# Beacon attention and soft MoE on one core: slot inputs always with x stationary, a later right half, wider zero fill, 0.72 weights a pair

## The chip, the cores and the metric

The kernel runs on one core of a Trainium2 chip. Its time is device microseconds of one execution. The engines are TensorE (PE, with its weight loads as PEld), VectorE (DVE), ScalarE (ACT), GpSimd (POOL) and SyncE (SP); sixteen DMA engines move data between HBM and the core's memory. SP and POOL issue transfers here: SP's go into the profile's queue q1 (hardware), POOL's into q0 (software).

## What is computed

Attention over 8 batches and 8 heads, 576 tokens of 64 columns, with 16 beacon keys and values that every token sees and a causal mask over the rest. Its output, with the heads side by side, is x: 4608 rows of 512. A soft mixture of 8 experts follows:

```python
x = np.ascontiguousarray(attn_out.transpose(0, 2, 1, 3)).reshape(B * S, H * D)
logits = x @ phi                                    # 4608 x 32 slots
d = np.exp(logits - logits.max(0)); d /= d.sum(0)   # over the tokens
slot_input = (d.T @ x).reshape(E, 4, 512)
for e in range(E):                                  # w1 512x1024, w2 1024x512
    slot_out[e] = np.maximum(slot_input[e] @ w1[e], 0.0) @ w2[e]
c = np.exp(logits - logits.max(1)); c /= c.sum(1)   # over the slots
return c @ slot_out                                 # 4608 x 512
```

## The kernel before, in words

**Pairs.** Attention goes over 32 pairs of heads (NP), four pairs to a batch. The order of the work is written out by hand: `lists[n]` (L583 to L598) names the pieces of pair n, `do` (L609) runs them, and each engine takes its instructions in that order. Q and K of a pair are transposed on PE and copied by DVE (`transp4`: Qa, Qb, Ka, Kb; `transp`: Ta, Tb). S0 to S3 (`score`) are the four steps of scores: products into one of two PSUM tiles sc, an exponential on ACT (L403) into ex, and masks on POOL (L387). M is a mask on DVE (L413). A0 and A1 (`attend`) multiply the pair before with V into av, of which there is one; after A1 DVE takes reciprocals (L434) and writes the normalized rows into xb (L435), two buffers of one batch each.

**Slots.** When a batch of x is done, X0, X12 and X34 transpose it (L471, L476), L0 and L1 form its logits and their exponentials (L486, L490), and D turns those into dT, tokens on the partitions (L540 to L544). SI adds d.T @ x of a batch, two batches behind the pair that runs it. In it batches 0 to 5 go through `si_moving` (L560): the 128x32 block of dT is stationary, 512 columns of x move, four row blocks go to four groups of 32 columns of PE, and one DVE instruction adds the 128x512 sum to siq (L568). In pair 30, SX (`si_turn`, L571) folds the four groups and transposes with eight fp32 products against the selector slc, and DVE writes siacc (L576). Batches 6 and 7 go through `si_piece` (L546): blocks of 128 columns of x are stationary, 32 columns of dT move, 20 products, and one DVE instruction adds the 128x128 sum to siacc, already transposed (L556); the last one writes siT, which the first expert layer takes.

**Loads.** SP loads q, k (`load_pair`, six pairs ahead, five buffers each) and v (`load_r`, `load_vl`). The weights are 32 blocks of 1 MB, cast from 32 to 16 bits on the way by transfers that POOL issues (`load_w`, L190): 27 whole tiles w, then ten pieces wx into the buffers that q and k have left, of which the last six hold the left halves and then the right halves of the last three blocks (L209). How many are issued by which pair is `want(n)` (L667), looked at before S0 of each pair (L698), and at D in the last. Before D of the last pair POOL clears hTz (L696), a view of one of the V buffers in which the transposed hidden rows are put later.

**End.** After the pairs: logits and slot inputs of the last batch, `layer1` with ReLU on ACT and DVE, `turn` (hidden rows transposed into hTz, L784), `layer2` for experts 0 to 5. `slot_out(hf)` (L797) does experts 6 and 7 for one half of the columns and writes soh (L800). `group(cg, o, w)` (L831) makes 512 output rows: per row block a product (L838), an eviction by ACT (L840) or DVE (L843), and a transfer of two row blocks at a time by SP (L847, L850). There are nine groups: the left halves of the first three, with slot_out(1) ahead of the third, then their right halves, then six groups of full width.

**Start.** `late_constants` (L317) clears siq (DVE, L318), builds slc (POOL, L319, L321) and ssel (POOL).

Of the kernel before, what the change touches and what calls it, by code (L numbers as in the profile page):

```python
# [8 lines left out]
FP = mybir.dt.float32  # L9
F16 = mybir.dt.float16  # L10
BF = mybir.dt.bfloat16
AL = mybir.AluOpType
# [5 lines left out]
def kernel(  # L18
# [12 lines left out]
    nc = tc.nc  # L31
    P = 128
    B, H, S, D = q.shape
    Nb = beacon_k.shape[2]
    E, Dm, F = moe_w1.shape
    NSL = moe_phi.shape[1]
# [3 lines left out]
    NCH = 5  # L40
    UL = U - 4 * P
    UE = (UL + Nb) // 2
    J = S // 64
    NP = B * H // 2
    NDC = Dm // P
# [31 lines left out]
    POS = [0, 2, 1, 3, 4]  # L77
# [9 lines left out]
    const = ctx.enter_context(tc.tile_pool(name="const", bufs=1))  # L87
# [87 lines left out]
    NV = NW + 3  # L175
    wv = {}
    homes = ["qf", "kf"] * 5
    NH = len(homes)
# [50 lines left out]
    def dcols(x, c):  # L229
        o = 2 * P * (c // 2) + c % 2  # L230
        return x[:, o:o + 2 * P - 1:2]
# [70 lines left out]
    siT = const.tile([P, NDC, NSL], F16, name="siT")  # L302


    siq = const.tile([P, Dm], FP, name="siq")
    slc = const.tile([P, NSL], FP, name="slc")


    ssel = const.tile([P, E // EG, EG * SPE], F16, name="ssel")
    phih = const.tile([P, NDC, 4, NSL], F16, name="phih")  # L310
    bkT = const.tile([P, NP, Nb], BF, name="bkT")
# [3 lines left out]
    scs = [ps_sc.tile([P, 2, 512], FP, name=f"sc{i}") for i in range(2)]  # L315

    def late_constants():  # L317
        nc.vector.memset(siq[:, :], 0.0)  # L318
        nc.gpsimd.memset(slc[:, :], 0.0)  # L319
        for c in range(P // NSL):  # L320
            nc.gpsimd.affine_select(out=slc[:, :], in_=slc[:, :], compare_op=AL.not_equal, fill=1.0,  # L321
                                    base=-NSL * c, pattern=[[-1, NSL]], channel_multiplier=1)
        nc.gpsimd.memset(ssel[:, :, :], 0.0)
        for gr in range(E // EG):
            for i in range(EG):
                nc.gpsimd.affine_select(
                    out=ssel[:, gr, i * SPE:(i + 1) * SPE], in_=ssel[:, gr, i * SPE:(i + 1) * SPE],
                    compare_op=AL.not_equal, fill=1.0,
                    base=-(NSL * i + (gr * EG + i) * SPE), pattern=[[-1, SPE]], channel_multiplier=1)
# [216 lines left out]
    def si_piece(b):  # L546
        sp = ps_tr.tile([P, NDC, NSL], FP, name="tr", tag="tr")
        for t in range(NDC):
            for i in (1, 2, 3, 4, 0):
                m = P if i < 4 else UL  # L550
                nc.tensor.matmul(
                    sp[:, t, :],
                    dcols(xb[b % 2][0:m, POS[i], :, :].rearrange("p h d -> p (h d)"), t),
                    dT[b][0:m, i, :], start=(i == 1), stop=(i == 0))

        nc.vector.scalar_tensor_tensor(  # L556
            out=siT[:, :, :] if b == B - 1 else siacc[:, :, :], in0=sp[:, :, :],
            scalar=2.0 ** -8, in1=siacc[:, :, :], op0=AL.mult, op1=AL.add)

    def si_moving(b):  # L560
        sp = ps_tr.tile([P, Dm], FP, name="tr", tag="tr")
        for i in range(NCH):
            m, c = P if i < 4 else UL, i % 4
            nc.tensor.matmul(  # L564
                sp[NSL * c:NSL * c + NSL, :], dT[b][0:m, i, :],
                xb[b % 2][0:m, POS[i], :, :].rearrange("p h d -> p (h d)"),
                start=i < 4, stop=i in (1, 2, 3, 4))
        nc.vector.scalar_tensor_tensor(out=siq[:, :], in0=sp[:, :], scalar=2.0 ** -8,  # L568
                                       in1=siq[:, :], op0=AL.mult, op1=AL.add)

    def si_turn():  # L571
        sp = ps_tr.tile([P, NDC, NSL], FP, name="tr", tag="tr")
        for t in range(NDC):
            nc.tensor.matmul(sp[:, t, :], dcols(siq, t), slc[:, :],
                             start=True, stop=True)
        nc.vector.tensor_copy(out=siacc[:, :, :], in_=sp[:, :, :])  # L576

# [13 lines left out]
    lists[NP - 5] = "S1 A0 L0 M S2 Ka Kb S3 A1 X34 e0 S0".split()  # L594
    lists[NP - 4] = "S1 A0 L1 M S2 Ta Tb S3 e1 A1 d1 S0".split()
    lists[NP - 3] = "S1 D A0 SI M S2 Ta Tb S3 A1 X0 S0".split()
    lists[NP - 2] = "S1 A0 X12 M S2 X34 A1 L0 S3 SX S0".split()
    lists[NP - 1] = "S1 A0 P0 M S2 P1 A1 L1 S3 D".split()  # L598
    routing = {"X0": lambda b: xt_piece(b, (0,)), "X12": lambda b: xt_piece(b, (1, 2)),
               "X34": lambda b: xt_piece(b, (3, 4)), "L0": lambda b: logit_piece(b, 0),  # L600
               "L1": lambda b: logit_piece(b, 1), "D": lambda b: dt_piece(b),
               "SI": lambda b: (si_moving if b < B - 2 else si_piece)(b)}


    def idle_work(t, m):
# [3 lines left out]
    def do(n, w):  # L609
        b, g = divmod(n, H // 2)  # L610
        if w in routing:
            rb = b - 1
            if w == "SI" or n < NP - 1 and w in ("L1", "D"):
                rb = b - 2
            if rb >= 0:
                routing[w](rb)
        elif w in ("Qa", "Qb", "Ka", "Kb"):
            transp4(n // 2 + 1, "QK".index(w[0]), "ab".index(w[1]))
        elif w[0] == "T":
            m, ws = (n + 2, ("ab".index(w[1]),)) if w[1] in "ab" else (int(w[1]), (0, 1))  # L620
            for x in ws:
                transp(m, x)
        elif w == "BC":
            beacon_cast(1, B)
        elif w == "BT":
            beacon_t(1, B)
        elif w == "M":
            mask_f(n)
        elif w == "SX":
            si_turn()  # L630
        elif w[0] == "P":
            xt_pair(int(w[1]))
        elif w[0] == "A":
            if n >= 1:
                attend(n - 1, int(w[1]))
        elif w == "S0":
            if n + 1 < NP:
                score(n + 1, 0)
        elif w[0] == "S":
            score(n, int(w[1]))  # L640
        elif w == "bv":
            cast_bv0()
        elif w[0] in "cde":

            vb = 0 if n < 2 else b if g == 0 else b + 1
            if vb >= B:
                pass
            elif w[0] == "e":
                cast_vl(vb, int(w[1]))
            elif w[0] == "c":  # L650
                cast_r(vb, int(w[1]), nc.vector if vb == 0 else nc.gpsimd)
            else:
                dup(vb, int(w[1]))
# [12 lines left out]

    def want(n):  # L667
        if n < 24:
            return max(0, int(0.75 * n - 0.8))
        return {24: 18, 25: 20, 26: 21, 27: 23, 28: 25, 29: NV, 30: NV + 3}.get(n, NV + NH)  # L670

    transp(0, 0, nc.scalar.copy)
    beacon_cast(0, 1)
# [10 lines left out]
    for n in range(NP):  # L684
        b, g = divmod(n, H // 2)
        if n + 2 < NP and n not in (2, 3):
            beacon_k_in(n + 2, nc.gpsimd)
        for w in lists[n]:
            if n == 3 and w == "M":
                beacon_k_in(n + 1, nc.gpsimd)  # L690
                beacon_k_in(n + 2, nc.gpsimd)
            if n == 6 and w == "M":
                for r in range(4):
                    nc.vector.tensor_copy(out=phih[:, :, r, :], in_=phif[:, :, :])
            if n == NP - 1 and w == "D":
                nc.gpsimd.memset(hTz, 0.0)  # L696
            if w == ("e0" if n == 3 else "D" if n == NP - 1 else "S0"):
                while wl < want(n):  # L698
                    load_w(wl)
                    wl += 1  # L700
            do(n, w)
        for what, vb in asks.get((n, 0), []):
            what(vb)
        for m in (5, 6) if n == 0 else (n + 6,):
            if m < NP:
                load_pair(m)
        for what, vb in asks.get((n, 1), []):
            what(vb)
# [119 lines left out]
    sc_scope.close()  # L828
    ps_f = ctx.enter_context(tc.tile_pool(name="ps_f", bufs=4, space=PSUM, side="right"))

    def group(cg, o, w):  # L831
        dst = out[cg * P * G:(cg + 1) * P * G, :].rearrange("(p j) d -> p j d", j=G)
        for j0 in range(0, G, 2):
            osb = wh.tile([P, 2, Dm], FP, name="osb", tag="w")
            for j in range(j0, j0 + 2):
                i = cg * G + j
                fp_ = ps_f.tile([P, Dm], FP, name="fp", tag="fp")
                nc.tensor.matmul(fp_[:, 0:w], etok(cg, j), soh[:, o:o + w], start=True, stop=True)  # L838
                if j % 2 == 0:
                    nc.scalar.activation(osb[:, j - j0, o:o + w], fp_[:, 0:w], AF.Copy,  # L840
                                         scale=rc[:, i:i + 1])
                else:
                    nc.vector.tensor_scalar(out=osb[:, j - j0, o:o + w], in0=fp_[:, 0:w],  # L843
                                            scalar1=rc[:, i:i + 1], scalar2=None, op0=AL.mult)

                if cg == 0 and o == 0 and j0 == 0:
                    nc.sync.dma_start(out=dst[:, j:j + 1, o:o + w],  # L847
                                      in_=osb[:, j - j0:j - j0 + 1, o:o + w])
            if cg > 0 or o > 0 or j0 > 0:
                nc.sync.dma_start(out=dst[:, j0:j0 + 2, o:o + w], in_=osb[:, :, o:o + w])  # L850


    NL = 3
    for cg in range(NL):
        if cg == NL - 1:
            slot_out(1)
        group(cg, 0, HD)
    for cg in range(NL):
        group(cg, HD, HD)
    for cg in range(NL, NG):  # L860
# [31 lines left out]
```

## Time and profile before

| | |
|---|---|
| runs, us | 194.15, 195.35, 202.19; median 195.35 |
| profiled execution, us | 195.3 |
| its span, us | 193.6 |
| granted TensorE clock | 0.972 |
| PE, DVE, ACT, POOL busy, us | 156.8, 146.6, 129.5, 119.1 |
| DMA | 56.11 MB as landed, mean 290 GB/s |

The span runs from the first to the last instruction of the profiled execution; times in the text without another name count from its start. In the groups a line is: line, engine, operation, out<-in with shapes and count, then for a source or tile view least, median and longest duration in ns. The busy share of the DMA engines is shown in tenths for 40 slices of the span, as a sum over transfers that may overlap on an engine, so that it can be above 1.

### The profile page before, as it was taken

Reading aid. Unit: us, or ns where it says so; the run is one execution under the profiler, and the core shown is the slowest. Engines: PE = TensorE matmul, PEld = TensorE weight load, DVE = VectorE, ACT = ScalarE, POOL = GpSimd, SP = SyncE. Lnnn points to the kernel's source line nnn. Section 1 sums busy time; section 2 is a strip of 40 time slices with the busy share of each in tenths; the row PEclk is TensorE's granted clock in tenths of the full one; section 3 lists DMA queues with packets and bytes.
Section 4 is the critical chain, followed back from the end, with each engine's and each line's share of the span. In section 5 each row is a group of like instructions: output and inputs, shape, how many; then the busy total and the mean of one; then the engine's idle time right before and its main releaser. Section 6 shows DMA issues by size and latency. Waiting matters only on the chain.

```text
span 193.6 us, 7169 instructions
## 1 busy us (share of the span) xinstructions
PE 156.8 (81%) x2985; PEld 110.3 (57%) x2985; DVE 146.6 (76%) x306; ACT 129.5 (67%) x190; POOL 119.1 (62%) x278
## 2 busy tenths in 40 slices
PE   2569996989998989999998999999889999688300
PEld 1327674666676756767665766677567867343000
DVE  3595999989898988889898987997776524599500
ACT  3474876878788878879877877888668131399400
POOL 7996597678478858856875888697756860000000
PEclk9999999999999999999999999999999999999855
DMA  5999999999999999999999999999999999999995
GB/s 182 324 334 367 374 349 294 290 325 242 282 275 346 285 260 314 312 305 263 370 287 271 299 295 311 259 261 225 215 216 212 210 203 197 198 362 407 419 420 232
DMA packets 45048, 56.11 MB, mean 290 GB/s; under 512 B 4191, under 2 KB 30295, under 8 KB 45015
## 3 DMA queue, kind: packets, MB, share of 16 engines
q1 hardware_dynamic: 36359, 38.87, 58.7%
q0 software_dynamic: 8656, 16.78, 46.5%
q8 instruction: 23, 0.38, 0.7%
q14 instruction: 10, 0.08, 0.1%
HBM read 62.98 MB, written 9.44 MB: 374 GB/s over the span
## 4 chain that ended last, share of the span: by engine, by line
DVE 48%; PE 26%; issue 6%; DMA 5%; POOL 4%; ACT 3%; DVEq 0%; POOLq 0%; ACTq 0%
DVE xb L435 12%; PE av L426 9%; DVE qT L377 9%; DVE kT L377 8%; DMA wx<-in_moe_w_dram 5%; PE sc L396 4%; PE tr L375 4%; PE tr L486 4%; DVE ex L413 3%; DVE osb L843 3%; DVE kT L362 2%; DVE siq L568 2%; DVE qT L362 2%; ACT ex L403 2%; PE tr L564 2%
## 5 line engine op out<-in xcount | busy, mean ns | idle before, releaser
L403 ACT ACTIVATE ex<-sc 128x928 f16<-128x928 f32 (+2 forms) x128 | 106.4, 868 | 28.0 <-PE sc L396 20.6
L387 POOL TENSOR_SCALAR_AFFINE_SELECT ex<-ex 128x256 f16<-128x256 f16 x128 | 51.3, 414 | 35.4 <-ACT ex L403 32.8
L426 PEld LDWEIGHTS <-ex 128*128 128x128 f16 (+1 forms) x960 | 42.2, 106 | 18.2 <-issue 17.5
L396 PE MATMUL sc<-qT,kT 64*64 64x128 bf16 (+3 forms) x640 | 46.1, 264 | 4.8 <-DVE kT L382 2.2
L426 PE MATMUL av<-vh,ex 128*128 128x65 f16 x819 | 42.1, 199 | 0.1
L396 PEld LDWEIGHTS <-kT 64*64 64x64 bf16 (+1 forms) x640 | 17.6, 104 | 20.9 <-issue 7.9
L426 PE MATMUL av<-vd,ex 128*128 128x130 f16 x126 | 21.9, 225 | 8.7 <-DVE xb L435 6.6
L435 DVE TENSOR_TENSOR xb<-av,r 128x640 f16<-128x640 f32 (+1 forms) x32 | 26.0, 814 | 1.1
L377 DVE COPY kT<-tr 128x640 bf16<-128x640 bf16 (+1 forms) x24 | 18.0, 772 | 4.0 <-PE tr L375 4.0
L377 DVE COPY qT<-tr 128x640 bf16<-128x640 bf16 (+1 forms) x24 | 17.5, 769 | 3.2 <-PE tr L375 3.2
L413 DVE TENSOR_TENSOR ex<-ex,fmask 128x672 f16<-128x672 f16 x32 | 19.1, 595 | 0.4 <-ACT ex L403 0.2
L840 ACT ACTIVATE osb<-fp,rc 128x256 f32<-128x256 f32 (+1 forms) x24 | 12.9, 579 | 7.3 <-PE fp L838 6.7
L441 POOL CAST vh<-vr 128x1024 f16<-128x1024 f32 x15 | 16.0, 1066 | 0.1
L843 DVE TENSOR_SCALAR osb<-fp,rc 128x256 f32<-128x256 f32 (+1 forms) x24 | 13.7, 614 | 0.7 <-PE fp L838 0.6
L457 POOL CAST vh<-vl 48x256 f16<-48x256 f32 x32 | 13.2, 413 | 1.3
L838 PE MATMUL fp<-soh,eLh 128*128 128x256 f16 (+1 forms) x48 | 11.4, 325 | 2.6 <-ACT osb L840 1.5
L476 DVE COPY xT<-tr 128x512 f16<-128x512 f16 (+1 forms) x21 | 10.6, 504 | 0.9 <-PE tr L471 0.9
L471 PE MATMUL tr<-idh,xb 128*128 128x128 f16 (+1 forms) x140 | 10.8, 215 | 0.4 <-DVE qT L377 0.4
L375 PE MATMUL tr<-idb,kf 128*64 128x128 bf16 x216 | 9.9, 224 | 0.8 <-DVE qT L377 0.8
L838 PEld LDWEIGHTS <-eLh 128*128 128x128 f16 x48 | 5.3, 114 | 8.3 <-issue 6.5
L486 PE MATMUL tr<-xT,phih 128*128 128x288 f16 x56 | 9.2, 286 | 0.0
L375 PEld LDWEIGHTS <-kf 128*64 128x64 bf16 x216 | 7.1, 109 | 3.5 <-issue 3.3
(122 smaller groups left out, 199.3 us busy)
## 6 DMA issues: line engine op xcount, KB each, us to landing
w<-in_moe_w_dram POOLq DMA_DIRECT2D x27, 512.0 KB, 8.8
qf<-in_q_dram SPq DMA_DIRECT2D x32, 288.0 KB, 7.4
kf<-in_k_dram SPq DMA_DIRECT2D x32, 288.0 KB, 6.2
vr<-in_v_dram SPq DMA_DIRECT2D x15, 512.0 KB, 6.6
out_dram<-osb SPq DMA_DIRECT2D x12, 512.0 KB, 5.7
out_dram<-osb SPq DMA_DIRECT2D x11, 256.0 KB, 3.0
wx<-in_moe_w_dram POOLq DMA_DIRECT2D x10, 256.0 KB, 9.8
vl<-in_v_dram SPq DMA_DIRECT2D x16, 96.0 KB, 10.2
```

The source lines that it names most:

```text
L375: nc.tensor.transpose(tp[64 * r:64 * r + 64, j - j0, :], ts[r][:, j, :].bitcast(BF)[:, 1::2], idb[:, :])
L377: nc.vector.tensor_copy(out=dst[:, :, Nb:Nb + S].rearrange("p a (s j) -> p a s j", j=J)[:, :, :, j0:j1], in_=tp[:, :, :].rearrange("p j (a ...
L387: nc.gpsimd.affine_select(out=x, in_=x, compare_op=AL.is_ge, fill=0.0, base=base, pattern=pattern, channel_multiplier=cm)
L396: nc.tensor.matmul(sc[p0:p0 + kn, a, col:col + un], kT[n // 2 % 2][64 * a:64 * a + 64, n % 2, k0:k0 + ks * (kn - 1) + 1:ks], qT[n // 2 % 2 ...
L403: nc.scalar.activation(x[:, :, o:o + w], sc[:, :, 0:w], AF.Exp, scale=scale)
L413: nc.vector.tensor_tensor(out=x, in0=x, in1=fmask[:, :].unsqueeze(1).broadcast_to([P, 2, XT + UL]), op=AL.min)
L426: nc.tensor.matmul(dst, ex[n][0:kn, a, o:o + m], rhs, start=j in first, stop=j in final)
L435: nc.vector.tensor_tensor(out=xb[b % 2][:, :, h0:h0 + dh * (na - 1) + 1:dh, :].rearrange("p i a d -> p a i d"), in0=avv[:, :, :, 0:D], in1 ...
L441: eng.tensor_copy(out=vh[b % 2][:, 2 * r:2 * r + 2, :, 0:D].rearrange("p s h d -> p h s d"), in_=vr.pop((b, r))[:, :, :].rearrange("p h (s ...
L486: nc.tensor.matmul(lp[:, 0:w], phih[:, t, :, :].rearrange("p r e -> p (r e)"), xT[b][:, t, Nb + hf * w:Nb + (hf + 1) * w], start=(t == 0), ...
L838: nc.tensor.matmul(fp_[:, 0:w], etok(cg, j), soh[:, o:o + w], start=True, stop=True)
L843: nc.vector.tensor_scalar(out=osb[:, j - j0, o:o + w], in0=fp_[:, 0:w], scalar1=rc[:, i:i + 1], scalar2=None, op0=AL.mult)
```

## The change

All batches take `si_piece`, so `si_moving`, `si_turn`, the piece SX and the constants siq and slc go, and POOL clears siacc at the start. hTz is cleared through a view of 32-bit words. `want` asks for 0.72 weights a pair where it asked for 0.75, and for one less at pairs 24 and 25. `group` takes the row blocks as an argument, and in the third left group slot_out(1) stands between its two halves.

```diff
-    siq = const.tile([P, Dm], FP, name="siq")
-    slc = const.tile([P, NSL], FP, name="slc")
     def late_constants():
-        nc.vector.memset(siq[:, :], 0.0)
-        nc.gpsimd.memset(slc[:, :], 0.0)
-        for c in range(P // NSL):
-            nc.gpsimd.affine_select(out=slc[:, :], in_=slc[:, :], compare_op=AL.not_equal, fill=1.0,
-                                    base=-NSL * c, pattern=[[-1, NSL]], channel_multiplier=1)
+        nc.gpsimd.memset(siacc[:, :, :], 0.0)
...
-    def si_moving(b):
...
-    def si_turn():
...
-    lists[NP - 2] = "S1 A0 X12 M S2 X34 A1 L0 S3 SX S0".split()
+    lists[NP - 2] = "S1 A0 X12 M S2 X34 A1 L0 S3 S0".split()
...
-               "SI": lambda b: (si_moving if b < B - 2 else si_piece)(b)}
+               "SI": lambda b: si_piece(b)}
...
     def want(n):
         if n < 24:
-            return max(0, int(0.75 * n - 0.8))
-        return {24: 18, 25: 20, 26: 21, 27: 23, 28: 25, 29: NV, 30: NV + 3}.get(n, NV + NH)
+            return max(0, int(0.72 * n - 0.8))
+        return {24: 17, 25: 19, 26: 21, 27: 23, 28: 25, 29: NV, 30: NV + 3}.get(n, NV + NH)
...
-                nc.gpsimd.memset(hTz, 0.0)
+                nc.gpsimd.memset(hTz.bitcast(FP), 0.0)
...
-    def group(cg, o, w):
+    def group(cg, o, w, js=range(0, G, 2)):
         dst = out[cg * P * G:(cg + 1) * P * G, :].rearrange("(p j) d -> p j d", j=G)
-        for j0 in range(0, G, 2):
+        for j0 in js:
...
     for cg in range(NL):
+        group(cg, 0, HD, (0,))
         if cg == NL - 1:
             slot_out(1)
-        group(cg, 0, HD)
+        group(cg, 0, HD, (2,))
```

More of the change, by code (lines that the diff above doesn't have):

```diff
@@ L558, in si_piece @@
             scalar=2.0 ** -8, in1=siacc[:, :, :], op0=AL.mult, op1=AL.add)
-    def si_moving(b):
[L561 to L569, printed above, removed]
-    def si_turn():
[L572 to L576, printed above, removed]
     order = ["S1 A0 L1 M S2 Qa Qb S3 A1 Ka S0", "S1 D A0 SI M S2 Kb S3 A1 X0 c0 S0",
@@ L628, in do @@
             mask_f(n)
-        elif w == "SX":
-            si_turn()
         elif w[0] == "P":
```

## The prediction

> **What bounds the kernel now.** I read the page first (queues, busy rows, chain), then busy time by stretch, then the chain and the timeline around one slot-input step and around the end.
>
> ```profile
> span 193.6 us, 7169 instructions
> DMA  5999999999999999999999999999999999999995
> q1 hardware_dynamic: 36359, 38.87, 58.7%
> q0 software_dynamic: 8656, 16.78, 46.5%
> HBM read 62.98 MB, written 9.44 MB: 374 GB/s over the span
> w<-in_moe_w_dram POOLq DMA_DIRECT2D x27, 512.0 KB, 8.8
> wx<-in_moe_w_dram POOLq DMA_DIRECT2D x10, 256.0 KB, 9.8
> ```
>
> Packets of the two queues fill 58.7% + 46.5% = 105% of sixteen engines' span, and the busy row is 9 in all slices but the first and the last. The weights' 16.78 MB are counted as they land, in 16 bits; they are read as 33.5 MB. The stretches (PE, PEld, DVE, ACT, POOL, then clock, DMA share, GB/s) say whether that is a limit:
>
> ```profile
> 28.00:118.00 90.00, 81.57 (x1589) 58.73 (x1589) 79.50 (x157) 72.84 (x104) 66.21 (x152) 1.00 1.08 297
> 136.00:156.00 20.00, 18.40 (x360) 14.38 (x358) 13.17 (x35) 11.59 (x20) 14.47 (x29) 1.00 1.07 213
> 156.00:165.00 9.00, 8.95 (x224) 5.90 (x221) 3.13 (x10) 1.19 (x2) 1.99 (x3) 1.00 1.35 197
> 165.00:168.00 3.00, 1.83 (x24) 1.19 (x21) 2.24 (x5) 1.68 (x4) 0.00 (x0) 1.00 0.91 157
> 168.00:171.00 3.00, 1.86 (x13) 1.13 (x13) 1.79 (x5) 1.72 (x4) 0.00 (x0) 1.00 0.89 306
> 171.00:192.00 21.00, 8.45 (x32) 3.38 (x30) 10.57 (x17) 9.55 (x17) 0.00 (x0) 0.78 1.02 399
> ```
>
> From 136 to 156 only weights move, at 213 GB/s landed, 426 read; they land every 2.45 us (a 512 KB tile) however they were issued, each 10 to 13 us after its issue, against 7.4 for the quickest tile: a queue that has fallen behind. From 28 to 118 the share is the same 1.08. So the transfers are saturated from about 2 us to 165, and compute, though PE and DVE take turns at nearly full time, only paces what is asked for. The last weight piece lands at 168.68; the output, 9.44 MB, leaves after. Both stretches around that point, 0.91 and 0.89, are the only slack. The chain agrees at its end:
>
> ```profile
> 153.01 0.55 POOL wx L214
> 153.57 1.43 POOL wx L209 x2
> 158.40 10.28 DMA wx<-in_moe_w_dram
> 168.72 0.29 PE tr L794 x4
> ```
>
> **The change, part by part.** The profiled execution took 195.3 us, 1.7 more than its span; the median of the three runs is 195.35, so the sum holds for either.
>
> *Slot inputs.* The chain around one step, and the rows of old and new form:
>
> ```profile
> 102.94 0.06 DVE dT L544
> 103.04 0.62 PE tr L564 x5
> 103.69 0.69 DVE siq L568
> 104.38 0.42 DVE ex L413
> 104.80 0.63 DVE kT L377
> 105.43 0.11 DVE r L434
> ```
> ```profile
> L551 PE MATMUL tr<-dT,xb x40: 176/176/181, 152.4 to 156.1; 128*128 128x32 f16 x32, 80*128 80x32 f16 x8
> L556 DVE SCALAR_TENSOR_TENSOR siacc<-tr,siacc x1: 281/281/281, 153.3 to 153.3; 128x128 f32<-128x128 f32 x1
> ```
>
> Six batches leave five matmuls and a 0.692 us addition for what two batches do already: 20 matmuls, which the timeline shows in 0.66 us from 152.37 (the last takes 0.176, so they start every 25 ns), and an addition of 0.281. PE: +0.04 a batch, 0.24 in all; DVE: -0.41 a batch, -2.47 in all. How much compute time is that? After the step PE goes on without a stop: S2, the second K transposes, S3, and the attention product whose last matmul ends at 105.25, while the reciprocal of L434 starts at 105.32, after DVE's copy. With 0.37 taken from DVE's side the reciprocal waits for PE instead, and gains at most 0.07 a batch, 0.4 us over six. What is late next is that product. And none of it reaches the end, since it only lets loads be asked for earlier, of engines that are full. If that cover were gone, 0.4 us is its worth. Taken: 0.
>
> The rule that speaks against this part: the Trainium skill, "TensorE: Matmul & The Clock Gate", section "LDWEIGHTS (loading the stationary operand)", gives a load its columns over 1.2 in ns, 107 here, so 20 would be 2.1 us a batch by an estimate, and six batches 9 us more PE time. The trace shows each load as 96 ns, but 20 of them with their products inside 0.66 us, so they overlap and the row decides.
>
> *The turn (SX) in the second to last pair* goes: eight fp32 products, 1.13 us of PE from 145.13, and a DVE copy of 0.29. The next scores then start at 145.2 instead of 146.19, but ACT is on another exponential until 146.28 and started theirs at 146.64: 0.36 us of compute. It meets the landing of the third left piece at 164.55, which PE reaches at 164.42; the four products that need it take 0.29, so the left product ends at about 164.9 instead of 165.04. Output starts 0.15 us earlier, in a stretch where engines are idle (share 0.91). Taken: -0.15; bounds 0 and -0.36.
>
> *Zero fills.* L696, 1.83 us for 2080 16-bit elements, becomes the shape of L294's 1040 words: 0.96 and 1.19, so -0.64 to -0.87 on POOL. Behind it wait seven weight issues, from 153.01. At that time a tile and three pieces were issued and still to land, the last at 159.27; and the tenth piece does not wait for POOL but for a landing (1.15 us of waiting until 158.40). Taken: 0; bounds 0 and -0.87. At the start, DVE's fill of 0.485 at 7.16 goes, ahead of 1.67 us of idle time: nothing. On POOL 0.12 + 4 x 0.213 = 0.97 becomes one fill of 128x128 words, between 0.12 (128x32) and 0.96 (128x1040), about 0.2: some 0.8 earlier for the first cast of V at 9.97. Queue full from 4 us on: 0; bounds 0 and -0.8.
>
> *0.72 weights a pair.* By the two formulas the totals are equal at pairs 3 to 7, 9, 10, 11, 13, 14, 17, 18, 21, 22 and from 26 on; at 8, 12, 15, 16, 19, 20, 23, 24 and 25 one tile is issued one pair (4.3 us) later. No load on SP is moved; POOL issues the same 37 DMAs, two at pair 26 instead of one. While a tile is missing, SP's loads have the engines: between 47 and 53 and between 79 and 83 they took 9 to 12 us to land against 6 when alone, so there is work to do in its place. If there were not, the worst is one tile's time, 2.45 us, at the end. A gain could come from q and k landing sooner, but no engine waits for them in the waits view after the first pairs. Taken: 0; bounds -0.3 (mixed stretches read up to 410 GB/s, SP's alone 365, over 3 us) and +2.45.
>
> *Right halves inside the third left group.* Two left products, their evictions and one 256 KB output move ahead of the wait for the last piece. Before, outputs are issued at 168.80, 170.00, 170.47; the two evictions can run at 167.7 to 168.3 (ACT and DVE sit idle from 167.8 to 169.06), and the issue comes at about 169.3. The twelve early right products move from 167.18 to about 167.5 and still end before 168.68, so soh is not later. In 0.15 us slices the DMA runs at 239, 55 and 218 GB/s from 170.55 to 171.0, against 380 just after: (0.37 + 0.86 + 0.43) x 0.15 = 0.25 us lost, which the extra transfer fills. After that outputs are transfer-bound (share 1.02 to 192). Taken: -0.25; bounds 0 and -0.5 (one issue interval of 0.47).
>
> Sum: 195.3 - 0.15 - 0.25 = **194.9 us**.
>
> **The rivals.**
> 1. *Compute is the bound after all.* The page's chain gives DVE 48%, PE 26% and DMA 5%, and has siq and the turn on it. Then -2.47 - 1.07 - 0.75 - 0.4 = -4.7: 190.6. Against it: the full share, and weights that land late in a row without any engine's wait.
> 2. *The late tiles cost* (the other side). If engines go idle while a tile is held back, at pairs 23 to 25 above all, that time is missing at 168.68: up to 2.45, less 0.4: 197.3. It decides from 0.4 us of idle on. For it: from 44 to 47 us, with few SP loads queued, the rate fell to 277 and 316 GB/s. Against: SP's backlog at 117 to 122 (14 us to land).
> 3. *The loads of x do not overlap in mid-kernel*: 20 x 96 ns = 1.92, 1.38 more than now; 8.3 over six. The weight queue's delay above its quickest, 12 - 7.4 = 4.6 us, absorbs as much; 3.7 remains: 199. Against: the same form at 152.
> 4. *It does nothing that shows*: the gaps at 165 to 171 move instead of closing: 195.3.
>
> **How the numbers follow.** Forecast 0.66, rival 1 0.06, rival 2 0.12, rival 3 0.03, rival 4 0.13. The runs spread from 194.15 to 195.35 without the highest, so 0.6 either way on any of them. Low end 193.2: the forecast with all its gains at their bounds in the tail (-0.36 - 0.5 - 0.3) less 0.9 of spread and of compute that does show. High end 196.6: half a tile lost (194.9 + 1.2) with half a microsecond of spread. Outside lie rivals 1 and 3 and half of 2. Two per cent, about what a measurement here tells from no change, is 3.9 us: faster means below 191.4, which only rival 1 gives (0.06); slower means above 199.3, the upper part of rival 3 and several lost tiles (0.03); the same 0.91.
>
> **What would show it.** Right: the last weight piece lands within 0.7 us of 168.7; tiles still land every 2.45 us from 136 to 155; the addition of each batch takes 0.28 us and the 20 products 0.66, yet four pairs still take 17.1 to 17.3 us (now 102.00 to 119.24); the reciprocal after a slot input waits for PE; the zero fill takes about 1.1; no dip in the output at 170.5. Wrong: the last landing earlier by 2 us or more (rival 1), SP-only stretches with a DMA share under 1 at pairs 23 to 25 and a later landing (rival 2), L551's groups above 1 us (rival 3).

## The result and the profile after

| | before | changed |
|---|---|---|
| median of runs, us | 197.19 (194.15 to 202.19, 6 runs) | 202.46 (201.75 to 203.15, 6 runs) |
| profiled execution and its span, us | 195.3, 193.6 | 203.15, 201.4 |
| granted TensorE clock | 0.972 | 0.948 |
| last weight lands, then to the end, us | 168.68, 24.9 | 175.86, 25.6 |

The ratio is 1.040 (95% interval 1.034 to 1.046): slower. Medians here are over all runs and ratios over the undisturbed ones, so that a ratio and the quotient of two medians can differ by 1%. The forecast was 194.9, with a range of 193.2 to 196.6.

Line numbers of the changed kernel are lower than those of the prediction: by 8 from L335 on (the beacons' cast), so that the cast of V is L433 for L441 and x L427 for L435, and by 28 in the last part (L766 for L794, L819 and L822 for L847 and L850). The page of the changed kernel, with the rows that the prediction showed of the other:

```profile
span 201.4 us, 7322 instructions
DMA  5999999999999999999999998999999999999996
q1 hardware_dynamic: 36359, 38.87, 60.4%
q0 software_dynamic: 8656, 16.78, 44.6%
HBM read 62.98 MB, written 9.44 MB: 359 GB/s over the span
w<-in_moe_w_dram POOLq DMA_DIRECT2D x27, 512.0 KB, 9.2
wx<-in_moe_w_dram POOLq DMA_DIRECT2D x10, 256.0 KB, 10.6
```

The bytes and the packets are the same to the last digit. What has grown is the time that SP's packets take: 58.7% of 193.6 us was 113.6 us an engine, 60.4% of 201.4 us is 121.6. These are 8.0 us more, and the span has grown by 7.8. POOL's packets take what they took, 46.5% of 193.6 = 90.0 us and 44.6% of 201.4 = 89.8. The stretches (PE, PEld, DVE, ACT, POOL, clock, DMA share, GB/s) say the same:

```profile
28.00:118.00 90.00, 81.31 (x1617) 60.17 (x1613) 76.22 (x153) 71.41 (x101) 65.44 (x153) 0.98 1.08 283
136.00:156.00 20.00, 17.43 (x384) 13.27 (x382) 14.36 (x33) 15.47 (x23) 14.79 (x36) 1.00 1.09 213
...
178.00:199.00 21.00, 8.33 (x31) 3.25 (x29) 10.12 (x17) 9.30 (x16) 0.00 (x0) 0.80 1.02 389
```

From 28 to 118 the DMA share is 1.08 as before, but 283 GB/s come of it and not 297. Where weights move almost alone, from 136 to 156, nothing has changed: 213 GB/s. In the output stretch 399 has become 389.

The trace has the duration of each packet. By size (SP's queue; mean, and the share of packets at or under the shortest common time):

| packet | what it is | before | changed |
|---|---|---|---|
| 512 B | v and its beacon rows, into vr and vl | 28.1 ns, 92% at 27 | 31.7 ns, 58% |
| 2304 B | q and k | 100.5 ns, 74% at 93 | 105.6 ns, 41% |
| 1024 B | half output rows | 46.4 ns, 98% at 46 | 48.8 ns, 70% |
| 4096 B | whole output rows, two a packet | 159.2 ns, 99% at 159 | 163.6 ns, 56% |

Weighted with their numbers (19960, 8192, 3072 and 1536) that is 4.5 + 2.6 + 0.5 + 0.4 = 8.0 us an engine again. Medians hardly move (27, 95 for 93, 46 and 159): the shortest time is as short as before, and fewer packets reach it. The engines' own buffers behind the constants moved too, but work on them did not get longer: an exponential into ex takes 868 ns in the mean in both kernels, a copy into xT 504.

Where the 8 us are felt shows by pairs, as the start of each pair's normalization of x against the trace of before. Pairs 0 to 2 are 1.0 to 1.2 us early. Pair 3 is 2.1 late, and from there to pair 22 the lag shrinks by 0.07 to 0.09 a batch, to 1.75. Pairs 23 and 24 lose 5.6, to 7.3, and of that 6.8 are left at pair 30. A wait stands at each of the two steps:

```profile
PE tr L367 <- DMA qf<-in_q_dram: 3.4, 1, 3.4
POOL vh L433 <- DMA vr<-in_beacon_v_dram: 3.1, 1, 3.1
```
```profile
108.34 13.36 DMA qf<-in_q_dram
121.75 0.69 PE tr L367 x17
...
164.75 11.11 DMA wx<-in_moe_w_dram
175.90 0.32 PE tr L766 x4
```

The waits are 3.1 of the 3.3 us lost at pair 3 and 3.4 of the 5.6. The rest of the second step falls where the granted clock was lower: 0.50 from 122.5 to 129.3 us. In the next fence (columns as above) three stretches are of the changed kernel, the last one of before:

```profile
118.00:122.00 4.00, 0.55 (x11) 0.36 (x11) 0.45 (x1) 1.20 (x3) 1.12 (x3) 1.00 1.06 302
122.00:124.00 2.00, 2.00 (x35) 1.48 (x32) 1.46 (x2) 0.94 (x1) 0.05 (x1) 0.62 0.56 166
124.00:129.00 5.00, 5.00 (x80) 3.33 (x79) 3.21 (x9) 2.43 (x3) 2.71 (x6) 0.50 1.10 314
...
124.00:129.00 5.00, 4.67 (x94) 3.41 (x91) 4.66 (x8) 4.11 (x6) 5.00 (x11) 1.00 1.11 267
```

PE was busy throughout the five microseconds and did 80 matmuls where it had done 94 in 4.67.

The chain above is the one that ended last. It has a load of q, for pair 27, in its middle, 13.36 us from issue to landing; before, the chain had no q load there. It was issued late, too: SP issues in order, and once a batch the load of the beacon rows (L152) stands ahead of the loads of q and k and must wait until the v load into the same buffer has landed. That wait of SP, before and changed (us in total, times, longest):

```profile
SPq L152 <- DMA vr<-in_v_dram: 6.3, 6, 2.4
```
```profile
SPq L152 <- DMA vr<-in_v_dram: 21.1, 5, 8.5
```

As the trace has it, slower packets make v land later, SP then issues q later, and that q is slow in its turn; no run isolates these links. The margin was small: before, the q of pair 27 landed 3.3 us ahead of its use; here 0.04, PE having waited for it. The last weight landed at 175.86, not within 0.7 us of 168.7 as the prediction's first sign asked.

### The profile page after: what moved, and what is told of

Same layout as the page of the kernel before. It is cut to its first block, busy times and chain, and to the rows that moved or that the text cites. A ratio compares the mean times of both kernels' runs of the same rounds, so it can differ in the third digit from the quotient of the medians.

```text
span 201.4 us, 7322 instructions
## 1 busy us (share of the span) xinstructions
PE 159.4 (79%) x3067; PEld 114.0 (57%) x3067; DVE 143.4 (71%) x304; ACT 129.3 (64%) x190; POOL 116.6 (58%) x274
## 3 DMA queue, kind: packets, MB, share of 16 engines
q1 hardware_dynamic: 36359, 38.87, 60.4%
q0 software_dynamic: 8656, 16.78, 44.6%
## 4 chain that ended last, share of the span: by engine, by line
DVE 31%; PE 31%; DMA 14%; issue 7%; POOL 6%; ACT 2%; DVEq 0%; SPq 0%; POOLq 0%; ACTq 0%
PE av L418 12%; DVE xb L427 10%; PE sc L388 7%; DMA qf<-in_q_dram 7%; DVE qT L369 6%; DMA wx<-in_moe_w_dram 6%; PE tr L367 5%; DVE kT L369 5%; PE tr L478 3%; DVE osb L815 2%; POOL ex L379 2%; PE tr L543 2%; DVE r L426 2%; DMA bk<-in_beacon_k_dram 2%; POOL wx L209 2%
## 5 line engine op out<-in xcount | busy, mean ns | idle before, releaser
L379 POOL TENSOR_SCALAR_AFFINE_SELECT ex<-ex 128x256 f16<-128x256 f16 x128 | 52.7, 427 | 40.5 <-ACT ex L395 37.9
L418 PEld LDWEIGHTS <-ex 128*128 128x128 f16 (+1 forms) x960 | 43.5, 109 | 20.4 <-issue 17.9
L388 PE MATMUL sc<-qT,kT 64*64 64x128 bf16 (+3 forms) x640 | 46.9, 267 | 5.9 <-ACT ex L395 2.0
L418 PE MATMUL av<-vh,ex 128*128 128x65 f16 x819 | 43.6, 201 | 1.9 <-POOL ex L379 1.8
L418 PE MATMUL av<-vd,ex 128*128 128x130 f16 x126 | 22.5, 229 | 8.5 <-DVE xb L427 6.9
L427 DVE TENSOR_TENSOR xb<-av,r 128x640 f16<-128x640 f32 (+1 forms) x32 | 26.1, 814 | 1.1
L433 POOL CAST vh<-vr 128x1024 f16<-128x1024 f32 x15 | 15.8, 1051 | 3.5 <-DMA vr<-in_beacon_v_dram 3.1
L810 PE MATMUL fp<-soh,eLh 128*128 128x256 f16 (+1 forms) x48 | 11.7, 324 | 2.7 <-ACT osb L812 1.4
L367 PE MATMUL tr<-idb,qf 128*64 128x128 bf16 x216 | 9.4, 230 | 3.4 <-DMA qf<-in_q_dram 3.4
L367 PEld LDWEIGHTS <-qf 128*64 128x64 bf16 x216 | 7.2, 115 | 6.3 <-DMA qf<-in_q_dram 3.6
L367 PE MATMUL tr<-idb,kf 128*64 128x128 bf16 x216 | 10.5, 231 | 0.0
```

The costliest lines, as they stand in the source:

```text
L367: nc.tensor.transpose(tp[64 * r:64 * r + 64, j - j0, :], ts[r][:, j, :].bitcast(BF)[:, 1::2], idb[:, :])
L379: nc.gpsimd.affine_select(out=x, in_=x, compare_op=AL.is_ge, fill=0.0, base=base, pattern=pattern, channel_multiplier=cm)
L388: nc.tensor.matmul(sc[p0:p0 + kn, a, col:col + un], kT[n // 2 % 2][64 * a:64 * a + 64, n % 2, k0:k0 + ks * (kn - 1) + 1:ks], qT[n // 2 % 2 ...
L418: nc.tensor.matmul(dst, ex[n][0:kn, a, o:o + m], rhs, start=j in first, stop=j in final)
L427: nc.vector.tensor_tensor(out=xb[b % 2][:, :, h0:h0 + dh * (na - 1) + 1:dh, :].rearrange("p i a d -> p a i d"), in0=avv[:, :, :, 0:D], in1 ...
L433: eng.tensor_copy(out=vh[b % 2][:, 2 * r:2 * r + 2, :, 0:D].rearrange("p s h d -> p h s d"), in_=vr.pop((b, r))[:, :, :].rearrange("p h (s ...
```

## The experiments

Ratios are to the kernel before on the same chip, with 95% intervals.

### The pace of the weights

e1 is the changed kernel with the old pace, e2 the kernel before with the new one:

```diff
-            return max(0, int(0.72 * n - 0.8))
-        return {24: 17, 25: 19, 26: 21, 27: 23, 28: 25, 29: NV, 30: NV + 3}.get(n, NV + NH)
+            return max(0, int(0.75 * n - 0.8))
+        return {24: 18, 25: 20, 26: 21, 27: 23, 28: 25, 29: NV, 30: NV + 3}.get(n, NV + NH)
```

> The changed kernel with the old pace of the weights alone put back (0.75, 18, 20); the rest of the change stays. Theory A, the pace: the moved tiles make the first V load of a batch land late, SP stands behind the beacon rows (21.1 us of such waits in the changed kernel, 6.3 before), q of pair 27 comes late. Then this kernel has no stall at pair 26 to 27, SP's wait for V is back under 9 us, and the time is that of the kernel before less 0.4 to 1: ratio 0.993 to 1.00. Theory B, the pace has no part and one of the other edits (POOL earlier at the start, another pattern on PE) sets off the stalls: ratio about 1.04.

> The kernel before with the new pace alone (0.72, 17, 19). Theory A: 1.025 to 1.045 of the kernel before, with a wait of PE for q of 2 us or more around pair 26 and over 15 us of SP's waits at the beacon rows. Theory B: 1.00 within 0.01.

e1 took 202.83, 1.034 (1.025 to 1.042); e2 196.49, 1.001 (0.996 to 1.005). The pace falls as the cause of the loss. e1 showed two such steps, 1.5 us late at pair 3 and 3.3 more at pair 22, and 11.7 us of SP's waits at the beacon rows.

### Beacon rows that need not wait

e3 is the changed kernel, e4 the one before; the first v load of a batch leaves out the eight partitions that the beacon rows fill:

```diff
-            nc.sync.dma_start(out=t[:, :, :], in_=vrows[o:o + H * S].rearrange(
-                "(h s) d -> h s d", s=S)[:, 0:2 * P, :].rearrange("h (p t) d -> p h (t d)", t=2))
+            nc.sync.dma_start(out=t[Nb // 2:P], in_=v[b, :, 0:2 * P - Nb, :].rearrange(
+                "h (p t) d -> p h (t d)", t=2))
```

> The changed kernel, but the first V load of each batch from 1 to 7 fills partitions 8 to 127 only, so that the beacon rows, which fill 0 to 7, need not wait for it and SP runs on. All that is used is still loaded. Theory A with SP's order as the link: the waits at the beacon rows vanish, q of pair 27 lands in time, and the stall of 3.6 us with what follows it is gone: 4 to 6 us faster than the changed kernel, ratio 0.99 to 1.02 to the kernel before. Rival C, it is q's own transfer that the weights slow down, whatever SP's order: still 1.03 to 1.045.

> The kernel before with the same V load (partitions 8 to 127). Theory A: in it SP loses 6.3 us at the beacon rows without any engine waiting for q, so 0.985 to 1.00; the spread of its runs (194 to 202) should shrink if that spread is the same stall now and then. Rival C: 1.00, the same spread.

Both became slower: 212.18, 1.077 (1.070 to 1.084), and 209.72, 1.063 (1.056 to 1.070). So the runs did not isolate SP's order: with this load other packets took longer too. In the one profile of e4, whose buffers lie as before, 512 B packets took 32.8 ns for 28.1 and those of q and k, whose loads were not changed, 114.4 for 100.5. Why they did, these runs do not show.

### The places of the buffers

The constants lie ahead of the buffers for loads in each partition's memory. siq (2048 B) and slc (128 B) were two of them, so without them everything behind moved down by 2176 B. In the built program the first q buffer was at 73,728 = 288 x 256 and is at 71,552 = 279.5 x 256; the v buffers went from 378 x 256 to 369.5 x 256, the weights' from 511 x 256 to 502.5 x 256. Buffer sizes are multiples of 256 (2304, 4096, 2048), so every buffer of q, k, v, weights and output rows began at a multiple of 256 before, and every one is 128 B off now. e5 and e6 add one tile that nothing uses, behind the last constant, to the changed kernel and to the one before:

```diff
     soh = const.tile([P, Dm], F16, name="soh")
+    pad = const.tile([P, 32], FP, name="pad")
```

> The changed kernel, with one unused tile of 128 bytes a partition after the last constant, and nothing else: every buffer that transfers write then begins 128 bytes later. Placement theory: the two dropped tiles (2,176 bytes a partition) moved every transfer buffer from an address divisible by 256 to one that leaves 128, and transfers into such places are slower from the first one on (in the changed kernel's trace 41% of the 2,304-byte packets take their usual 93 ns, before 74%; 57% of the 512-byte ones take 27 ns, before 92%). The pad makes the places divisible by 256 again, so the time comes back to 193.5 to 196 us (ratio 0.98 to 1.00), with packet shares as before and no stall at pairs 3 and 22. Rival, the work itself (products with x stationary, POOL starting 1 us earlier, the other order of the first output groups): instructions are the same, so it stays at 201 to 204 us (ratio 1.03 to 1.045).

> The kernel before, with the same unused tile of 128 bytes: its transfer buffers now begin at addresses that leave 128 on division by 256, and nothing of the change is in it. Placement theory: 200 to 204 us (ratio 1.02 to 1.045), shares of packets at their shortest time as in the changed kernel. Rival, the work itself: 195 to 198 us (ratio 0.995 to 1.005).

e5: 197.17, 1.003 (0.998 to 1.008). e6: 203.68, 1.030 (1.019 to 1.040). So 128 unused bytes take the loss away from the changed kernel and bring it to the one before, with nothing else of the change in it. A lower granted clock over the whole span is not the cause: in the profiled executions of e5 and e6 it was 0.956 and 0.957, with spans of 196.5 and 200.6 us. e6 in the page and the waits:

```profile
span 200.6 us, 7169 instructions
...
q1 hardware_dynamic: 36359, 38.87, 61.2%
```
```profile
SPq L152 <- DMA vr<-in_v_dram: 15.0, 7, 3.6
```

SP's packets took 61.2% of 200.6 = 122.8 us an engine, with 53% of the 512 B ones at 27 ns; pair 22 lost 4.0 us. In e5 they took 58.6% of 196.5 = 115.1, with 91%, and no wait stood at pairs 22 to 24:

```profile
span 196.5 us, 7322 instructions
...
q1 hardware_dynamic: 36359, 38.87, 58.6%
```

At pair 3 e5 still lost 1.7 us, which its expectation had ruled out, and its 197.17 lies above the 196 expected.

Next, which places count. e7 puts the pad behind the small tiles, so that only the 24 weight buffers (the later output rows) are at multiples of 256 again; e8 has it in both places, so that only q, k and v are:

```diff
+    spad = sml.tile([P, 32], FP, name="spad", tag="spad", bufs=1)
     hs = [exq.tile([P, F], F16, name="hs", tag="ex") for _ in range(E // EG)]
```

> The changed kernel with the 128 bytes put after the small tiles instead, so that only the 24 weight buffers (which later hold the output rows too) move to addresses divisible by 256; q, k and v still land 128 bytes off. Placement theory, if the weights' places are what counts (they are 60% of the written bytes and come in parallel to everything): 194 to 198 us. If the places of q, k and v count: 200 to 203 us, with the packets of 512 and 2,304 bytes still slow and those of 4,096 bytes (output rows) back at 159 ns. Rival, the work itself: 201 to 204 us.

> The changed kernel with 128 bytes after the constants and 128 more after the small tiles: q, k and v land at addresses divisible by 256, the 24 weight buffers 128 bytes off. The complement of the run before: if the places of q, k and v count, 194 to 197 us; if those of the weights count, 200 to 203 us, with the output packets of 4,096 bytes still slow; if each has its part, both of these runs lie between 196 and 201 us. Rival, the work itself: 201 to 204 us.

e7: 202.14, 1.028 (1.019 to 1.036). e8: 199.29, 1.015 (1.007 to 1.022).

| | 512 B at 27 ns | q, k at 93 | 1024 B at 46 | 4096 B at 159 | SP's packets, us an engine |
|---|---|---|---|---|---|
| before | 92% | 74% | 98% | 99% | 113.7 (summed from the packets) |
| e7 | 63% | 45% | 98% | 99% | 120.8 |
| e8 | 94% | 72% | 53% | 55% | 116.1 |

By its share at the shortest time each kind of packet follows the place of its own buffer, as a target (v, q, k) and as a source (output rows). Most of the packet time is in q, k and v. That the output rows' places cost the kernel time is not shown: e8 was expected at 194 to 197 us if the loads alone count and took 199.29, but its interval and that of e5, which has all places right, overlap (1.007 to 1.022, 0.998 to 1.008). The means of q and k are less steady than the shares: with their buffers at multiples of 256 they lay between 99.8 ns (e14) and 104.1 (e8), off them between 105.0 and 107.5 (the changed kernel, e1, e6, e7, e10). The weights' own packets, which POOL issues, kept 89 to 91 us an engine in both. Two more offsets: e10 is the kernel before with 64 B, e11 the changed one with v and the weights at multiples of 512 (128 B behind the constants, 256 behind the small tiles):

> The kernel before with an unused tile of 64 bytes after the constants: every transfer buffer 64 bytes off a multiple of 256. Placement theory, if only multiples of 256 are fast: 201 to 205 us as with 128 bytes (ratio 1.025 to 1.045). If the loss grows with the finer offset: over 205 us. If an offset of 128 is bad for a reason of its own: 195 to 198 us.

> The changed kernel with 128 bytes after the constants and 256 after the small tiles: v and the 24 weight buffers then begin at multiples of 512 (in the kernel before the weight buffers leave 256), half of q and k too. If a multiple of 256 is all that counts: the time of the run with the same places as before, within 0.5%. If multiples of 512 are better still: 1 to 3 us less than that, and a version that beats the kernel before.

e10: 205.05, 1.047 (1.037 to 1.056), SP's packets 122.8 us an engine as with 128 B. e11: 198.05, 1.012 (1.005 to 1.019), packets 114.4. So multiples of 512 brought no gain over those of 256: e5 had 1.003, and e9 below, at the places of before, 1.004. (e11 was expected within 0.5% of e9 and lies 0.8% above it; the intervals overlap.) An offset of 64 is no better than one of 128. Whether it is worse is open: e10 is just above the range expected for the same loss, but its interval overlaps that of e6, and its packets took no longer in sum.

### The work alone

e9 and, once more, e13 give the changed kernel a tile of 2176 B where the two dropped ones lay, so that every buffer has its address of before; e12 has the old pace besides:

```diff
+    pad = const.tile([P, 544], FP, name="pad")
     ssel = const.tile([P, E // EG, EG * SPE], F16, name="ssel")
```

> The changed kernel with one unused tile of 2,176 bytes a partition where the two dropped tiles lay, so that every buffer has exactly the address that it has in the kernel before: what is left is the work of the change alone. The working on record gave that -0.4 us (194.9 against 195.3, ratio 0.998). Placement theory: ratio 0.990 to 1.005. Rival, that part of the loss is the work (POOL's earlier start and the wait for the beacon rows at pair 3, or the order of the output groups): ratio 1.01 or more, with the wait at pair 3 that the run with 128 bytes still showed (1.3 us).

> The changed kernel with every buffer at its address of before (an unused tile of 2,176 bytes) and the weights at the pace of before (0.75, 18, 20): the new products, zero fills and group order alone. In the trace of before the last weight lands at 168.68 and the span ends 24.9 us later; in that of the kernel before with the new pace it lands at 169.29, although the pairs end 0.67 us earlier. If the new pace gives back in the last weights what the products save: the last weight lands by 169 us here, and the ratio is 0.988 to 1.000, about 0.5% below the run with the new pace beside it. Rival, the pace is worth nothing either way (as the two runs with one pace exchanged had it): the same ratio as beside it within 0.3%, about 1.004.

> The changed kernel with every buffer at its address of before, once more, beside the run with the old pace on the same chip. Its first profile was taken while TensorE's clock was granted at 0.588 over the whole span, and shows nothing of the order of the waits. Placement theory: ratio 1.000 to 1.006, span 194 to 196.5 us, no wait at pairs 22 to 24; the wait for the beacon rows at pair 3 may stand (0 to 1.5 us). If part of the loss were the work: over 1.01.

e9: 196.88, 1.004 (1.000 to 1.008). e13: 197.96, 1.010 (1.006 to 1.015). e12, beside e13: 197.32, 0.998 (0.993 to 1.002). (Before had 196.15 in that session.) The ratios of e9 and e13 are 0.036 and 0.029 below that of the changed kernel (1.040), which differs from them in addresses alone. e13 reached the 1.01 above which its expectation had part of the loss in the work. e12 and e13 differ in the pace alone, and the intervals do not meet: 0.0127 x 196.15 = 2.5 us. Against e9, the same kernel in another session, it is 0.0065 or 1.3 us, and there they overlap. PE's wait for the late weights, in e13 and in e12:

```profile
PE av L767 <- DMA wx<-in_moe_w_dram: 2.0, 2, 1.0
```
```profile
PE av L767 <- DMA wx<-in_moe_w_dram: 1.0, 1, 1.0
```

That is 1 us of the 2.5. In e13 the last weight lands 3.3 us later than in the first profile of before, though pair 30 is only 0.8 late; in e12 it is 2.9 and 1.3, so at 171.6 and not by 169 as expected. The two profiled executions took 198.87 and 198.59 us, so their traces hold little of the difference. Two more runs: the new products alone on the kernel before, both old tiles kept and filled (e14), and the kernel before itself (e15):

```diff
     def late_constants():
         nc.vector.memset(siq[:, :], 0.0)
+        nc.gpsimd.memset(siacc[:, :, :], 0.0)
...
-               "SI": lambda b: (si_moving if b < B - 2 else si_piece)(b)}
+               "SI": lambda b: si_piece(b)}
```

(SX is taken out of its list as well.)

> The kernel before with the new slot inputs alone: x stationary for every batch, the zeroed sum on POOL (0.2 us more there at the start), no turning step; both old tiles stay and are still filled, the pace and the output groups are those of before, and no address moves. Working on record for this part: 0.07 to 0.09 us a batch and 0.15 us once, less what the transfers hide. If it is worth what it says: ratio 0.990 to 1.000. If the wait for the beacon rows at pair 3, which every form of the changed kernel showed (1.3 to 2.3 us) and neither good form of the one before, comes of the constants' earlier end on POOL: it is not there in this run (under 0.7 us). If it comes of the products' form or of the program as such: 1.3 us or more here too, and the ratio is 1.00 to 1.01.

> The kernel before, unchanged, for a second profile of it: whether the first one's lack of a wait for the beacon rows at pair 3, and its 0.742 of q and k packets at 93 ns, are the kernel's or one execution's. If they are the kernel's: no wait over 1 us there, share 0.68 to 0.84, span 192.5 to 195.5 us. If one execution's: a wait of 1 to 2.5 us, and a span of 194 to 197.

e14: 197.43, 1.004 (0.999 to 1.008). Its pairs came from 1.1 us behind at pair 5 to 0.1 at pair 30, and its last weight landed at 169.10, 0.4 later than before. The gain is there pair by pair and gone at the end. At pair 3 it did not wait for the beacon rows. That would fit the earlier end of the constants on POOL as the cause of that wait, but e13, which has it, started its first pairs 0.6 us late and waited there (1.2 us). What e14 lost early, 1.3 us at pair 4, falls where the granted clock was 0.50, from 33.6 to 37.0 us; no load was waited for.

e15 met neither of its expectations. There was no wait at pair 3, 72% of the q and k packets took 93 ns, and yet this one execution took 203.38, where the others of the kernel in that session had 194.3 to 198.5. Its chain:

```profile
114.63 17.31 DMA qf<-in_q_dram
```

One q load, that of pair 29, took 17.31 us, PE waited 6.3 for it, and pair 26 was 8.5 late. In the changed kernel the late load was that of pair 27. So the kernel before can stall near the same place, with its buffers at multiples of 256; what held this load up is not known.

## Why the prediction was wrong, step by step

*The transfers are the bound* (first part): right in the main. The share from 28 to 118 was 1.08 before and after. Where the loads lay off, the span grew by about what SP's packets took more: 7.8 us for 8.0 in the changed kernel, 7.0 for 9.2 in e6, 6.8 for 7.1 in e7. It is no fixed price: in e8 it was 4.7 for 2.5, and in e15 8.1 for 0.4. Behind the stall at pair 23 the changed kernel's transfers were not full (0.56 from 122 to 124 us, a sign of rival 2, here behind a late q and not a late weight tile). The prediction measured the load of the queues and took the price of a packet as given.

*Zero fills, and siq and slc going*: this is the step that failed. The prediction costed the two constants by the instructions that filled them, "Taken: 0", and not by the 2176 bytes that they held. Those bytes kept the buffers of q, k, v, weights and output rows at multiples of 256. The edit that looked like clearing up costs 3 to 4%: e6 has it alone (1.030), and e1 against e12 has it at the old pace (1.034 and 0.998). No rival named it. Beside the rows stands a rule that would have: the Trainium skill, "DMA: Bandwidth & Descriptors", section "How a descriptor splits into AXI transactions", says that a transaction must start at a multiple of 256 B, so that a transfer that begins elsewhere starts at the one below and pays for bytes that nobody uses. By an estimate from that page of the Trainium skill, an offset of 128 B costs 512 B packets 20 beats for 16 (+25%), 1024 B ones +12.5%, q and k +5.6%, 4096 B ones +3.1%. The trace of the changed kernel is near it for the long ones (+5.1% for q and k, whose mean is unsteady, and +2.7% for 4096 B), shows half for the short ones (+13 and +5%), and differs in two points: many packets keep their shortest time, so it is no fixed price of each packet, and 64 B, which by the Trainium skill is half of the extra, cost 512 B packets as much (32.2 ns, and 32.1 in e6). The Trainium skill speaks there of what is fetched; e7 shows it for what is written as well.

The durations of the fills themselves were as forecast, in the changed kernel's groups:

```profile
L314 POOL MEMSET siacc<- x1: 194/194/194, 7.5 to 7.5; 128x128 f32 x1
```
```profile
L668 POOL MEMSET vd<- x1: 964/964/964, 158.0 to 158.0; 128x1040 f32 x1
```

The first pairs did start about 1 us earlier, and gave it back at once: POOL's cast of V at pair 3 waits for the beacon rows, so "queue full: 0" fits this part.

*Slot inputs*: right that they do not show in the time. An addition takes 0.28 to 0.29 us, 20 products 0.66 to 0.68 (0.72 once, at the lower clock):

```profile
L543 PE MATMUL tr<-dT,xb x160: 176/176/215, 53.2 to 162.9; 128*128 128x32 f16 x128, 80*128 80x32 f16 x32
L548 DVE SCALAR_TENSOR_TENSOR siacc<-tr,siacc x7: 281/292/292, 53.9 to 160.1; 128x128 f32<-128x128 f32 x7
```

Five of the six batches run 0.07 to 0.09 us faster, where the working had at most 0.07. The sixth brings 0.37, seen at pair 28 in the changed kernel and in e14, so that six are worth some 0.77 us of compute and not 0.4. In that step DVE worked without a pause from the addition to the reciprocal, so all that the addition saves shows; before:

```profile
138.28 0.69 DVE siq L568
138.97 0.58 DVE ex L413
139.55 0.67 DVE qT L362
140.22 0.67 DVE kT L362
140.88 0.14 DVE r L434
```

That nothing of it reaches the end fits e14 (1.004, 0.999 to 1.008). Rival 3 (loads of x that do not overlap, 199) does not hold: its time was the nearest, its mechanism absent. (Its 1.38 us a batch should have been 1.92 - 0.62 = 1.30.)

*The turn*: 0.15 us came off the lag at pair 30, in the changed kernel and in e14, where the working had 0.36 of compute. The 0.15 that it gave for the end is too small for these runs.

*The pace*: taken as 0, with 2.45 as the worst. On the kernel before it is 0 (e2, 1.001), on the changed one with the addresses of before 2.5 us (e12 beside e13) or 1.3 (e12 against e9). So rival 2, the late tiles, may be a second and smaller part of the loss; that engines go idle while a tile is held back, its mechanism, is not shown. Why the two forms differ in it was not settled; e13's weights fell further behind its pairs (2.5 us from pair 30 to the last landing) than e2's (1.3).

*Right halves in the third group*: the gap closed as forecast; in slices of 0.15 us from 175.9 to 180.4 the DMA share never falls below 0.83, where it had fallen to 0.16 at 170.7. It is a quarter of a microsecond, not seen in the times.

*The sum*: 194.9 against 195.3 is 0.998. With the addresses of before and the pace apart the same work measures 0.998 (0.993 to 1.002). That agreement is partly luck, since it leaves the pace out, and with it the same work measures 1.004 and 1.010; the interval does not tell a gain of 0.4 us from none either. What the sum lacked is the term that decided, the buffers' places. No version here beats the kernel before: the best is e12, level with it.

Left open: the first v load lands at 8.3 and 8.9 us in the first profiles of the good forms of before, at 8.9 to 10.1 in all forms of the changed kernel, also with equal addresses, and at 9.0 and 9.2 in e15 and e14. Whether that is the change or chance the runs do not tell. By itself it does not settle whether pair 3 waits for its beacon rows: in e8 it landed at 8.93, against 8.86 before, and pair 3 waited 3.1 us. The granted clock was 0.50 for 3.4 to 6.9 us between 28 and 38 us in every kept profile but the first of before and e2's (in e9's it was low over the whole span). That and the wait at pair 3 may be the rest of what e9 and e13 lack; the runs do not separate them.

## What to carry to other kernels

When an edit adds or drops a tile, look up where the transfer buffers behind it now begin, and keep them at multiples of 256 bytes with an unused tile if need be; in this kernel, bound by transfers, a miss of 64 or 128 bytes cost 3 to 5%. A profile tells it by the duration of packets of one size: same bytes, same DMA share, fewer GB/s, and the share of packets at the shortest time down by 28 to 43 points here. A step is costed by its bytes and where they lie, not by its instructions alone.

## What the runs showed of the hardware that was not expected

- The place of a buffer matters to packets in both directions: v, q and k into it, output rows out of it (e7, e8). Packets that POOL's queue moved took 89 to 91 us an engine in e5 to e8, wherever their buffers lay. Nor did the beacon keys' 256 B packets mind: their buffer lay 128 B off before and at a multiple of 256 in the changed kernel, and they took 18.0 ns in both.
- In the changed kernel the granted clock was 0.50 for 6.8 us behind PE's wait of 3.4 us for q, in e15 for 6.9 us around the end of its wait of 6.3. The late load cost more than the wait: 5.6 and 7.7 us by the pairs.
- With the first v load of seven batches over 120 partitions in place of 128 other loads were slower as well: q and k packets took 114.4 ns in e4 where they had taken 100.5, and the kernel lost 6%.
- 20 products with their own loads of x take 0.66 to 0.68 us also in mid-kernel at full clock, though a load by itself shows as 96 ns.
